# A decode-attention kernel: row loads at the start, the output weights at the end of the stream, fewer score matmuls, and prefetch two heads ahead

## The chip, the cores and the metric

The kernel runs on one core of one Trainium2 chip. The metric is the device time of a run in microseconds (us), as the median of several runs. The profile shows one execution of the same program; its span, from the first to the last instruction, is about 1 to 2 us shorter than the time of the run.

Engines in the profile: PE is the matmul engine and PEld its weight loads, DVE is VectorE, ACT is ScalarE, SP is the engine that issues most DMA transfers. DMA is done by 16 DMA engines, each of which carries a part of every large transfer.

## The reference

One token attends to a long cache, and a small gated MLP ("mixer") is mixed in. Shapes: 32 heads, 16384 cached positions, head size 128, model size 512, all bf16.

```python
q = (x @ wq).reshape(1, 1, 32, 128).transpose(0, 2, 1, 3)
scores = einsum('bhqd,bhkd->bhqk', q, k_cache) * 128 ** -0.5
o = einsum('bhqk,bhkd->bhqd', softmax(scores), v_cache)
a = o.transpose(0, 2, 1, 3).reshape(1, 1, 4096) @ wo
b = mixer(B_x, w_in, w_sp, b_sp, w_out)      # gelu, layernorm, two small products
g = sigmoid((x * gate_w).sum(-1, keepdims=True))
return g * a + (1 - g) * b
```

The two caches are 134 MB each and are read once. There is one query row, so almost no arithmetic is done per byte.

## The kernel before

Each head has a k tile and a v tile of 128 x 16384 bf16 (4.19 MB): partition p holds 128 positions. Scores are made on VectorE and PE together: VectorE multiplies half a k tile by q in place, PE sums over the head size by streaming the products past an identity matrix (16 matmuls of 512 columns per half), and VectorE adds up the last 8 columns. ScalarE takes the exponential. Attention is 128 one-column matmuls with v as weights.

```python
    x_col = const.tile([P, DC], BF16, name="x_col")
    gw_col = const.tile([P, DC], BF16, name="gw_col")
    nc.scalar.dma_start(out=x_col[:], in_=A_x.rearrange("b s (c p) -> p (b s c)", p=P))   # 2-byte pieces
    nc.scalar.dma_start(out=gw_col[:], in_=gate_w.rearrange("(c p) -> p c", p=P))
    ...
    def scores(h):
        ...
        for s in range(2):
            ks = k3[:, s * NH:(s + 1) * NH, :]
            nc.vector.tensor_tensor(out=ks, in0=ks, in1=qh, op=ALU.mult)
            s_ps = ps_s.tile([P, NH, W], FP32, name="s_ps")
            for i in range(NS):                                   # NS = 16
                nc.tensor.matmul(s_ps[:, :, :], lhsT=ident[:, :], rhs=ks[:, :, i * W:(i + 1) * W], ...)
            nc.vector.tensor_reduce(out=s_sb[...], in_=s_ps[:, :, :], axis=AX.X, op=ALU.add)
    ...
    def attend(h, dst):
        for j in range(NJ):                                       # NJ = 128
            nc.tensor.matmul(dst, lhsT=v3[:, j, :], rhs=p_sb[h][:, j:j + 1], ...)

    for h in range(H):          # k and v: two buffers each; k one head ahead
        ...
        if h == 6:
            nc.sync.dma_start(out=wo[:], in_=A_wo.rearrange("(h p) n -> p h n", p=P))
        scores(h)
        if h < last:
            attend(h, o_ps[:, h:h + 1])
    ...                          # softmax sums; o_sb = o * g / sum
    for h in range(last):
        nc.tensor.matmul(a_ps[:, :], lhsT=o_sb[:, h:h + 1], rhs=wo[:, h, :], ...)   # 512 columns each
    attend(last, o31_ps[:, :])
    ...                          # scale, one more wo matmul, copy, store
```

(Cuts are marked by dots.)

The softmax here doesn't subtract the row's maximum and nothing guards it: scores larger than these inputs give would overflow.

## Time and profile before

| | before |
|---|---|
| time, median of 6 runs | 686.27 us (685.47 to 688.01) |
| span of the profiled run | 683.7 us |
| bytes moved | 280.3 MB |
| PE busy, VectorE busy | 424 us (62%), 330 us (48%) |

The first view is the table of stretches: for each stretch its length, then busy time and count of PE, PEld, DVE, ACT and POOL, the granted PE clock (1.00 is full speed), the DMA share (mean busy share of the 16 DMA engines) and GB/s.

```profile
0.00:20.00 20.00, 0.00 (x0) 0.10 (x1) 0.81 (x6) 1.28 (x1) 0.70 (x6) 1.00 0.94 365
20.00:40.00 20.00, 0.00 (x0) 0.00 (x0) 0.00 (x0) 0.00 (x0) 0.00 (x0) 1.00 0.99 421
40.00:50.00 10.00, 5.01 (x20) 2.00 (x20) 2.45 (x3) 1.40 (x4) 0.00 (x0) 1.00 0.98 380
50.00:60.00 10.00, 10.00 (x48) 4.48 (x46) 7.76 (x3) 4.21 (x6) 0.00 (x0) 1.00 0.54 210
200.00:600.00 400.00, 255.58 (x3328) 144.32 (x3328) 204.36 (x82) 8.45 (x42) 0.00 (x0) 0.72 1.00 430
620.00:640.00 20.00, 13.04 (x160) 7.19 (x160) 10.73 (x5) 0.40 (x2) 0.00 (x0) 0.67 0.91 379
660.00:665.00 5.00, 4.33 (x134) 3.53 (x131) 0.64 (x1) 0.00 (x0) 0.00 (x0) 1.00 0.85 345
665.00:670.00 5.00, 3.44 (x9) 1.34 (x10) 0.85 (x4) 0.40 (x2) 0.00 (x0) 0.56 0.15 61
670.00:683.70 13.70, 10.54 (x154) 5.58 (x152) 0.84 (x2) 0.00 (x0) 0.00 (x0) 0.75 0.00 1
```

In the middle the DMA share is 1.00 at 430 GB/s while PE and VectorE have time to spare. At 50 to 60 us the DMA is half idle, and after 670 us there is no DMA.

The list of waits (who waited for whom: us in total, times, longest) names the cause of the first hole, and the timeline of PE (start, length, instruction, count, idle time before it) shows the end.

```profile
PE g_ps L109 <- DMA gw_col<-in_gate_w_dram: 45.0, 1, 45.0
```

```profile
667.19 9.44 PE L233 MATMUL a_ps<-wo,o_sb 128*1 128x512 bf16 x31 [0.95 <-DVE o_sb L231]
676.56 3.40 PE L203 MATMUL o_ps<-p_t,v_t 128*128 128x1 bf16 x128
680.21 0.58 PE L238 MATMUL a_ps<-wo,o 128*1 128x512 bf16 x1 [0.25 <-DVE o L237]
```

The first matmul of the kernel waited 45 us for a load of 1 KB in two-byte pieces, and everything else on PE stood behind it. At the end, 9.4 us of wo matmuls and 3.4 us of attention run when the stream is over.

Three groups of instructions carry the argument about scores (line, engine, operation, shapes, count, then busy us and mean ns, then the idle time before them):

```profile
L191 PE MATMUL s_ps<-k_t,ident 128*128 128x512 bf16 x1024 | 291.3, 454 | 166.2 <-DVE k_t L188 166.2
L188 DVE TENSOR_TENSOR k_t<-k_t,qb 128x8192 bf16<-128x8192 bf16 x64 | 280.4, 4421 | 148.9 <-DMA k_t<-in_A_k_cache_dram 148.8
L193 DVE TENSOR_REDUCE s_sb<-s_ps 128x64 f32<-128x512 f32 x64 | 44.2, 691 | 138.4 <-PE s_ps L191 138.3
```

### The profile page before, as it was taken

The numbers are of one execution on the slowest core, as the hardware profiler recorded it, in microseconds if no ns is written. First come the engines' busy times: TensorE is split into PE (matmuls) and PEld (weight loads), VectorE is DVE, ScalarE is ACT, GpSimd is POOL, SyncE is SP. The second block draws the span as 40 slices with busy tenths as digits, with TensorE's granted clock in tenths as the row PEclk, the third lists the DMA queues.
The fourth block names the chain that finished last, engine by engine and source line by source line (L and its number), as shares of the span: only waits on it lengthen the run. The fifth ranks groups of instructions, "written<-read, shape, count | busy, mean of one in ns | idle before, by whom it ended". The sixth has DMA issues, their size and how long they took to land.

```text
span 683.7 us, 11025 instructions
## 1 busy us (share of the span) xinstructions
PE 424.2 (62%) x5255; PEld 233.8 (34%) x5255; DVE 330.1 (48%) x157; ACT 24.1 (4%) x80; POOL 0.7 (0%) x6
## 2 busy tenths in 40 slices
PE   0038788776176665566666665676665666666677
PEld 0014444432132333333333333343333333333343
DVE  0028565455055555443555554345555543555650
ACT  0012200000000000000000000000000000000000
POOL 0000000000000000000000000000000000000000
PEclk9998676676576677767677677776777667777796
DMA  8998999999999999999999999999999999999980
GB/s 339 431 372 336 428 436 429 436 428 392 438 433 430 430 430 432 427 436 430 429 426 428 427 430 428 429 431 430 432 430 431 430 428 434 428 429 388 417 367 2
DMA packets 17119, 280.29 MB, mean 410 GB/s; under 512 B 2481, under 2 KB 7474, under 8 KB 8242
## 3 DMA queue, kind: packets, MB, share of 16 engines
q1 hardware_dynamic: 15730, 279.58, 96.0%
q8 instruction: 41, 0.67, 0.4%
q10 hardware_dynamic: 1344, 0.00, 0.1%
q14 instruction: 4, 0.03, 0.0%
HBM read 279.58 MB, written 0.00 MB: 409 GB/s over the span
## 4 chain that ended last, share of the span: by engine, by line
DMA 59%; PE 27%; DVE 12%; issue 1%; ACT 0%; SPq 0%; ACTq 0%; DVEq 0%
DMA k_t<-in_A_k_cache_dram 52%; PE s_ps L191 23%; DVE k_t L188 11%; DMA gw_col<-in_gate_w_dram 6%; PE o_ps L203 1%; PE a_ps L233 1%; PE q_ps L121 1%; PE a_ps L176 0%; DVE s_sb L193 0%; SPq L78 0%; ACT L145 0%; ACT p_t L196 0%; DVE res L241 0%; PE ltot_ps L225 0%; PE tot_ps L153 0%
## 5 line engine op out<-in xcount | busy, mean ns | idle before, releaser
L191 PE MATMUL s_ps<-k_t,ident 128*128 128x512 bf16 x1024 | 291.3, 454 | 166.2 <-DVE k_t L188 166.2
L188 DVE TENSOR_TENSOR k_t<-k_t,qb 128x8192 bf16<-128x8192 bf16 x64 | 280.4, 4421 | 148.9 <-DMA k_t<-in_A_k_cache_dram 148.8
L191 PEld LDWEIGHTS <-ident 128*128 128x128 bf16 x1024 | 115.2, 113 | 330.4 <-issue 209.9
L203 PE MATMUL o_ps<-p_t,v_t 128*128 128x1 bf16 x4096 | 109.1, 164 | 38.6 <-ACT p_t L196 38.6
L203 PEld LDWEIGHTS <-v_t 128*128 128x128 bf16 x4096 | 109.2, 98 | 51.7 <-issue 48.0
L193 DVE TENSOR_REDUCE s_sb<-s_ps 128x64 f32<-128x512 f32 x64 | 44.2, 691 | 138.4 <-PE s_ps L191 138.3
L196 ACT ACTIVATE p_t<-s_sb 128x128 bf16<-128x128 f32 x32 | 9.9, 309 | 574.4 <-DVE s_sb L193 574.4
L109 PE MATMUL g_ps<-gw_col,xb 128*128 128x1 bf16 x4 | 0.2, 166 | 45.0 <-DMA gw_col<-in_gate_w_dram 45.0
L109 PEld LDWEIGHTS <-xb 128*128 128x128 bf16 x4 | 0.3, 107 | 44.9 <-issue 27.7
L164 DVE CAST wbf<-wb 128x2 f32<-128x2 bf16 x1 | 0.2, 169 | 30.0 <-DMA wb<-in_B_b_sp_dram 30.0
L233 PE MATMUL a_ps<-wo,o_sb 128*1 128x512 bf16 x31 | 9.4, 478 | 1.0 <-DVE o_sb L231 1.0
L121 PE MATMUL q_ps<-wq_t,xb 128*128 128x512 bf16 x32 | 8.6, 429 | 0.0
L106 DVE COPY xb<-x_col 128x128 bf16<-128x128 bf16 x4 | 0.6, 222 | 15.8 <-DMA x_col<-in_A_x_dram 15.8
L237 DVE TENSOR_TENSOR o<-o_ps,rl 128x1 bf16<-128x1 f32 x1 | 0.2, 160 | 12.9 <-PE o_ps L203 12.9
L196 ACT ACTIVATION_READ_ACCUMULATOR p_t<-s_sb 128x1 f32 x32 | 6.0, 186 | 0.0
L233 PEld LDWEIGHTS <-o_sb 128*1 128x1 bf16 x31 | 3.0, 100 | 7.0 <-issue 3.8
L121 PEld LDWEIGHTS <-xb 128*128 128x128 bf16 x32 | 3.4, 108 | 4.8 <-issue 2.2
L176 PE MATMUL a_ps<-w_out,u 128*1 128x512 bf16 x7 | 3.3, 618 | 2.3 <-DVE u L173 2.3
L126 ACT CAST qb<-q_ps 128x512 bf16<-128x512 f32 x7 | 4.1, 585 | 4.7 <-PE q_ps L121 4.7
L196 ACT ACT_TABLE_LOAD x2 | 2.6, 1283 | 17.6 <-DVE s_sb L193 17.6
L153 PE MATMUL tot_ps<-stats,ones_f 128*128 128x2 f32 x2 | 0.6, 362 | 2.0 <-DVE stats L151 2.0
L176 PEld LDWEIGHTS <-u 128*1 128x1 bf16 x7 | 0.5, 100 | 3.3 <-DVE u L173 2.4
(43 smaller groups left out, 16.3 us busy)
## 6 DMA issues: line engine op xcount, KB each, us to landing
k_t<-in_A_k_cache_dram SPq DMA_DIRECT2D x32, 4096.0 KB, 25.4
v_t<-in_A_v_cache_dram SPq DMA_DIRECT2D x31, 4096.0 KB, 29.8
wq_t<-in_A_wq_dram SPq DMA_DIRECT2D x1, 4096.0 KB, 13.7
wo<-in_A_wo_dram SPq DMA_DIRECT2D x1, 4096.0 KB, 40.8
v_t<-in_A_v_cache_dram SPq DMA_DIRECT2D x1, 2048.0 KB, 24.8
w_in<-in_B_w_in_dram SPq DMA_DIRECT2D x1, 1792.0 KB, 31.4
v_t<-in_A_v_cache_dram SPq DMA_DIRECT2D x1, 1024.0 KB, 27.5
v_t<-in_A_v_cache_dram SPq DMA_DIRECT2D x2, 512.0 KB, 28.1
```

What stands on the lines that cost most here:

```text
L106: nc.vector.tensor_copy(out=xb[:, c, :], in_=x_col[:, c:c + 1].broadcast_to([P, P]))
L109: nc.tensor.matmul(g_ps[:, :], lhsT=xb[:, c, :], rhs=gw_col[:, c:c + 1], start=(c == 0), stop=(c == DC - 1))
L121: nc.tensor.matmul(q_ps[:, :], lhsT=xb[:, c, :], rhs=wq[:, c, nb * QB:(nb + 1) * QB], start=(c == 0), stop=(c == DC - 1))
L126: nc.scalar.copy(out=qb[:, nb * QB:(nb + 1) * QB], in_=q_ps[:, :])
L153: nc.tensor.matmul(tot_ps[:, :], lhsT=ones_f[:, :], rhs=stats[:, :], start=True, stop=True)
L176: nc.tensor.matmul(a_ps[:, :], lhsT=u[:, c:c + 1], rhs=w_out[:, c, :], start=(c == 0), stop=False, skip_group_check=True)
L188: nc.vector.tensor_tensor(out=ks, in0=ks, in1=qh, op=ALU.mult)
L191: nc.tensor.matmul(s_ps[:, :, :], lhsT=ident[:, :], rhs=ks[:, :, i * W:(i + 1) * W], start=(i == 0), stop=(i == NS - 1))
L193: nc.vector.tensor_reduce(out=s_sb[:, s * NH:(s + 1) * NH], in_=s_ps[:, :, :], axis=AX.X, op=ALU.add)
L196: nc.scalar.activation(out=p_t[:], in_=s_sb[:], func=ACT.Exp, scale=inv_sqrt_dh, accum_out=L_sb[:, h:h + 1])
L203: nc.tensor.matmul(dst, lhsT=v3[:, j, :], rhs=p_sb[h][:, j:j + 1], start=(j == 0), stop=(j == NJ - 1))
L233: nc.tensor.matmul(a_ps[:, :], lhsT=o_sb[:, h:h + 1], rhs=wo[:, h, :], start=False, stop=False, skip_group_check=True)
```

## The change

It does five things: (1) x, gate_w and two scalars come as single rows and are spread over the partitions by small matmuls; (2) wq, w_in, w_out and wo are laid out so that each partition reads one long line; (3) VectorE adds the two halves of the head before the identity matmuls, which halves them; (4) k runs two heads ahead in three buffers; (5) wo is loaded last, in five pieces, behind the last v, and is used as weights in one-column matmuls. Small moves go with these: the gate and the mixer come one head earlier in the program, and the last v takes a k buffer and comes in three pieces instead of four.

```diff
-        nc.scalar.dma_start(out=x_col[:], in_=A_x.rearrange("b s (c p) -> p (b s c)", p=P))
-        nc.scalar.dma_start(out=gw_col[:], in_=gate_w.rearrange("(c p) -> p c", p=P))
+    nc.scalar.dma_start(out=x_row[:], in_=A_x.rearrange("b s d -> (b s) d"))
+    nc.scalar.dma_start(out=gw_row[:], in_=gate_w.rearrange("(a d) -> a d", a=1))
 ...
-    nc.sync.dma_start(out=wq, in_=A_wq.rearrange("(c p) n -> p c n", p=P))
+    nc.sync.dma_start(out=wq_t[:], in_=A_wq.rearrange("(p c) n -> p (c n)", c=DC))
 ...
-        t = kv.tile([P, NJ * Dh], BF16, name="k_t", tag="k")
+        t = kv.tile([P, NJ * Dh], BF16, name="k_t", tag="k", bufs=3)
 ...
+        nc.tensor.matmul(xb_ps[:, c * P:(c + 1) * P], lhsT=x_row[0:1, c::DC], rhs=ones_row[0:1, :], ...)
 ...
-            for i in range(NS):
+            nc.vector.tensor_tensor(out=ks[:, :, 0:Dh // 2], in0=ks[:, :, 0:Dh // 2],
+                                    in1=ks[:, :, Dh // 2:Dh], op=ALU.add)
+            for i in range(NS // 2):
 ...
+    AHEAD = 2
+    scores(0)
+    scores(1)
     for h in range(H):
+        if h + AHEAD < H:
+            if h > 0:
+                load_k(h + AHEAD)
+            scores(h + AHEAD)
+        if h > 0:
+            load_v(h, cuts=(64, 96) if h == H - 1 else ())
+        if h < H - 1:
+            attend(h)
 ...
+    wo_src = A_wo.rearrange("(p k) n -> p (k n)", k=H)
+    for a, b in ((0, 12), (12, 20), (20, 26), (26, 30), (30, 32)):
+        nc.sync.dma_start(out=wo_t[:, a * D:b * D], in_=wo_src[:, a * D:b * D])
 ...
-    for h in range(last):
-        nc.tensor.matmul(a_ps[:, :], lhsT=o_sb[:, h:h + 1], rhs=wo[:, h, :], ...)
-    attend(last, o31_ps[:, :])
+    attend(H - 1)
+    ...                                  # two small transposes put o into wo's row order
+    for k in range(H):
+        for c in range(DC):
+            nc.tensor.matmul(a_ps[:, c:c + 1], lhsT=wo4[:, k, c, :], rhs=o2[:, k:k + 1], ...)
+    ...                                  # one small transpose, copy, store
```

## The prediction

> **What bounds the kernel now.** The DMA. The table of stretches shows about 430 GB/s and a DMA share of 1.00 from 200 to 600 us, with PE busy 62 to 65%, VectorE 51%. The Trainium skill ("DMA: Bandwidth & Descriptors", "Where 436 GB/s comes from") puts the ports' ceiling at 435 GB/s; the trace agrees within about 1%. The bytes do not change: 280 MB at 430 GB/s need 652 us. The span is 683.7 us, so about 32 us are lost:
> 1. Start, about 10 us. The two-byte gathers are slow (x_col lands after 16.1 us, gw_col after 43.6). The first matmul waits for gw_col until 45.0 us (list of waits), q follows, the big buffers stay full, and DMA falls to 67 GB/s in 50 to 55 us.
> 2. Middle, about 3 us: 402 GB/s in 160 to 180 us (wo in 1 KB pieces), 349 in 630 to 640.
> 3. End, about 18 us. DMA is done by about 666 us; then follow 9.4 us of wo matmuls, 3.4 us of attention, small work, 2.2 us of output.
>
> The chain of waits says 59% DMA, 27% PE, 12% VectorE; in the middle that is a buffer-recycling loop hidden behind the full DMA queue.
>
> **What the change does.**
> - Start: rows of 1 KB instead of gathers. q starts when wq lands (about 14 us), done by about 23, when k0 lands. scores(0) frees its buffer near 40 us, needed near 59. The hole vanishes: minus 7 us.
> - Middle: wo leaves it, lines become longer: minus 1 to 3 us.
> - End: wo comes last, behind v31. Attention of head 31 and the transposes hide under its 9.7 us (4.19 MB at 430). After its last piece: 8 one-column matmuls (27 ns each, from attention's 109.1 us for 4096), two copies, a transpose, the output: about 4 us instead of 18, minus 14 us.
> - Scores: 512 matmuls of 512 columns go (145 us of PE, off the critical path). VectorE gets 64 adds of 128x4096. A 128x8192 multiply takes 4.42 us, a tiny op 0.15, so an add is an estimated 2.3 us, again two elements per cycle ("VectorE: DVE Perf Modes", "The perf-mode tier table"; the multiply agrees). Plus 147 us: VectorE about 475 us, 72%. Per head 2 x (4.42 + 2.29 + 0.69) = 14.8 us, plus up to 3.5 us waiting for the second half's matmuls: 18.3 us, against 19.5 us of DMA per head. Hidden, with little slack.
> - Prefetch: k runs two heads ahead in three buffers: robustness, no bandwidth, as the queue was never dry in the middle.
>
> **Sum.** 652 us of streaming + 3 start + 1 for small pieces at the end + 4 after the last byte = 660 us span; run times are about 1 to 2 us above the span: **661 us**, 0.963 of before. Range 656 to 671 us. Chances: faster 0.88, same 0.08, slower 0.04.
>
> **What would show it.** DMA share about 1.0 from 5 us until the last 6 us, no slice between under 400 GB/s; first q matmul at 14 to 15 us; adds of 2.2 to 2.4 us; last DMA landing about 4 us before the end; VectorE near 475 us, its idle before multiplies still ended by k loads.
>
> **What would make it wrong.** If VectorE runs multiply, add, wait, reduce strictly in series (2 x 11 = 22 us per head), or attention gets between a head's score matmuls, VectorE passes 19.5 us per head and sets the pace: 700 us or more. Adds at one element per cycle (4.4 us) would do the same. If the deeper queue lifts the rate to 435, about 653 us.

## The result

| | before | after |
|---|---|---|
| time, median | 686.27 us (16 runs, 685.47 to 688.45) | 663.78 us (8 runs, 663.70 to 664.11) |
| span of the profiled run | 683.7 us | 662.4 us |
| PE busy | 424 us | 306 us |
| VectorE busy | 330 us | 472 us |
| bytes moved | 280.3 MB | 280.2 MB |

The 16 runs of the kernel before contain the 6 above. The ratio is 0.9668, 95% interval 0.9657 to 0.9679. Here and below a ratio is the mean time of one kernel's fast runs over the mean of the other's from the same rounds, so it is not quite the ratio of the medians that are quoted. 661 was predicted, within 656 to 671.

The table of stretches of the kernel after, columns as before:

```profile
0.00:20.00 20.00, 7.30 (x29) 3.21 (x30) 2.33 (x10) 3.62 (x5) 0.70 (x6) 1.00 0.94 392
20.00:40.00 20.00, 7.21 (x34) 2.96 (x33) 17.16 (x7) 4.55 (x7) 0.00 (x0) 0.74 0.98 423
40.00:50.00 10.00, 3.33 (x8) 1.09 (x8) 10.00 (x7) 0.40 (x2) 0.00 (x0) 0.83 1.05 452
50.00:60.00 10.00, 4.88 (x13) 1.68 (x13) 10.00 (x5) 0.40 (x2) 0.00 (x0) 0.69 1.00 423
200.00:600.00 400.00, 184.78 (x3013) 111.98 (x3012) 293.32 (x123) 8.57 (x42) 0.00 (x0) 0.63 1.00 430
640.00:650.00 10.00, 5.46 (x202) 5.29 (x198) 0.20 (x1) 0.00 (x0) 0.00 (x0) 0.54 1.00 414
650.00:655.00 5.00, 3.14 (x91) 2.88 (x91) 0.60 (x3) 0.00 (x0) 0.00 (x0) 0.50 0.58 237
655.00:660.00 5.00, 2.96 (x81) 2.52 (x81) 0.16 (x1) 0.00 (x0) 0.00 (x0) 0.50 0.27 104
660.00:662.40 2.40, 0.08 (x1) 0.00 (x0) 0.21 (x1) 0.00 (x0) 0.00 (x0) 0.50 0.00 0
```

The hole at 50 to 60 us is gone and the middle still runs at 430 GB/s. But from 650 us the DMA runs at half and then at a quarter of its rate for 9 us. That was not predicted.

The groups that answer to those of before, with the adds (L217) as a new one:

```profile
L220 PE MATMUL s_ps<-k_t,ident 128*128 128x512 bf16 x512 | 183.1, 535 | 328.8 <-DVE k_t L217 328.8
L215 DVE TENSOR_TENSOR k_t<-k_t,qb 128x8192 bf16<-128x8192 bf16 x64 | 280.4, 4421 | 56.1 <-DMA k_t<-in_A_k_cache_dram 56.1
L217 DVE TENSOR_TENSOR k_t<-k_t 128x4096 bf16<-128x4096 bf16 x64 | 143.7, 2283 | 0.0
L222 DVE TENSOR_REDUCE s_sb<-s_ps 128x64 f32<-128x512 f32 x64 | 44.1, 691 | 87.0 <-PE s_ps L220 87.0
```

An add takes 2.28 us, as estimated, and the multiplies still wait for k loads, though less (56 us instead of 149).

The end, on PE's timeline:

```profile
639.43 2.46 PE L232 MATMUL o_ps<-p_t,v_t 128*128 128x1 bf16 x90
644.26 3.57 PE L232 MATMUL o_ps<-p_t,v_t 128*128 128x1 bf16 x128 [2.37 <-issue]
650.46 1.17 PE L232 MATMUL o_ps<-p_t,v_t 128*128 128x1 bf16 x38 [2.62 <-issue]
653.05 1.42 PE L278 MATMUL a_ps<-o,wo_t 128*128 128x1 bf16 x48 [0.28 <-DVE o L275]
655.40 1.01 PE L278 MATMUL a_ps<-o,wo_t 128*128 128x1 bf16 x32 [0.93 <-DMA wo_t<-in_A_wo_dram]
657.28 0.80 PE L278 MATMUL a_ps<-o,wo_t 128*128 128x1 bf16 x24 [0.86 <-DMA wo_t<-in_A_wo_dram]
658.54 1.01 PE L278 MATMUL a_ps<-o,wo_t 128*128 128x1 bf16 x24 [0.47 <-DMA wo_t<-in_A_wo_dram]
659.81 0.27 PE L283 MATMUL rT_ps<-ident,res_col 128*4 128x128 bf16 x1 [0.25 <-DVE res_col L281]
```

The wo matmuls now follow the arrival of wo's pieces, and 3.3 us lie between the last landing (659.1 us) and the end of the span.

Why does the DMA thin out? A transfer reports one completion per DMA engine, and the trace has the time of each. The 16 completions of the last piece of wo in the kernel after, sorted (us from the start of the span):

```
first eight:  650.73 650.76 650.80 650.90 651.08 651.29 651.53 652.94
last eight:   656.80 656.89 656.99 658.55 658.58 658.62 658.62 659.13
```

Half of the DMA engines are done some four to eight us before the other half. Over the run the spread between the first and last completion of one transfer grows: 0.9 us for a transfer that lands at 56 us, 2.4 at 128, 4.0 at 285, 6.9 at 492, 8.4 at the end. The queue is never dry, so the early half runs ahead, and the late half decides when the stream ends. The kernel before has the same drift (0.6 us at 50 us, 8.1 at 638 us) but only 3.9 us at its end: across its DMA dip at 620 to 640 us the spread falls from 8.1 us (landing at 638 us) to 3.3 us (landing at 648 us), so the late half caught up there.

The drift goes in steps, and the trace shows what they follow. Besides the data it has DMA packets of kind "instruction", in which the engines fetch their instructions: 38 of 16 KB on one queue (q8) and, within the span, four of 8 KB on another (q14). For some transfers of the kernel after: first completion (us), packets of 16 KB and of 8 KB that had started by then, and by how much the late completions came after the first (us):

```
 57.73   0, 0   none late, all 16 within 0.86
 67.43   1, 0   2.42, the other 15 within 0.50
 77.14   2, 0   1.91 2.41, the others within 0.48
106.29   3, 1   1.45 1.90 1.99 2.41, the others within 0.43
183.97   8, 1   1.44 1.70 1.78 1.89 1.90 1.94 1.96 2.01 2.44, the others within 0.40
193.69   9, 1   1.44 1.70 1.77 1.90 1.90 1.93 1.97 2.00 3.98, the others within 0.39
```

Each 16 KB packet makes one completion about 1.5 us later, and it stays late in all transfers that follow. Eight packets hit eight different completions (the ninth late value, 1.44, is of the 8 KB packet), and the ninth packet hits one of the eight for the second time (3.98). Five such turns and the 0.9 us of the beginning make the 8.4 us of the end.

### The profile page after: what moved, and what is told of

Read it like the earlier page. It is cut to its first block, busy times and chain, and to the rows that moved or that the text cites. A ratio compares the mean times of both kernels' runs of the same rounds, so it can differ in the third digit from the quotient of the medians.

```text
span 662.4 us, 10310 instructions
## 1 busy us (share of the span) xinstructions
PE 305.7 (46%) x4875; PEld 185.6 (28%) x4875; DVE 471.5 (71%) x227; ACT 25.5 (4%) x81; POOL 0.7 (0%) x6
## 2 busy tenths in 40 slices
DMA packets 10714, 280.24 MB, mean 423 GB/s; under 512 B 1198, under 2 KB 1200, under 8 KB 1712
## 4 chain that ended last, share of the span: by engine, by line
DMA 61%; DVE 23%; PE 14%; SPq 1%; issue 0%; ACT 0%; DVEq 0%
DMA k_t<-in_A_k_cache_dram 55%; DVE k_t L215 17%; PE s_ps L220 9%; DVE k_t L217 5%; PE o_ps L232 5%; DMA v_t<-in_A_v_cache_dram 3%; DMA wo_t<-in_A_wo_dram 3%; DVE s_sb L222 0%; SPq L87 0%; PE z_ps L163 0%; PE tot_ps L180 0%; SPq L68 0%; PE a_ps L278 0%; ACT rstd L188 0%; DVE z2n L193 0%
## 5 line engine op out<-in xcount | busy, mean ns | idle before, releaser
L220 PE MATMUL s_ps<-k_t,ident 128*128 128x512 bf16 x512 | 183.1, 535 | 328.8 <-DVE k_t L217 328.8
L220 PEld LDWEIGHTS <-ident 128*128 128x128 bf16 x512 | 65.4, 128 | 434.5 <-issue 413.8
L217 DVE TENSOR_TENSOR k_t<-k_t 128x4096 bf16<-128x4096 bf16 x64 | 143.7, 2283 | 0.0
L278 PE MATMUL a_ps<-o,wo_t 128*128 128x1 bf16 x128 | 4.2, 166 | 2.6 <-DMA wo_t<-in_A_wo_dram 2.3
L278 PEld LDWEIGHTS <-wo_t 128*128 128x128 bf16 x128 | 3.9, 104 | 2.9 <-DMA wo_t<-in_A_wo_dram 2.8
L163 PEld LDWEIGHTS <-w_in 128*128 128x128 bf16 x56 | 3.2, 153 | 0.5 <-issue 0.5
L163 PE MATMUL z_ps<-xb,w_in 128*128 128x1 bf16 x56 | 3.1, 192 | 0.0
```

The lines of the kernel that those rows point to most:

```text
L163: nc.tensor.matmul(z_ps[:, fc:fc + 1], lhsT=w_in5[:, c, fc // FhC, :, fc % FhC], rhs=xb[:, c, 0:1], start=(c == 0), stop=(c == DC - 1))
L217: nc.vector.tensor_tensor(out=ks[:, :, 0:Dh // 2], in0=ks[:, :, 0:Dh // 2], in1=ks[:, :, Dh // 2:Dh], op=ALU.add)
L278: nc.tensor.matmul(a_ps[:, c:c + 1], lhsT=wo4[:, k, c, :], rhs=o2[:, k:k + 1], start=False, stop=(k == H - 1), skip_group_check=True)
```

## The experiments

Two sets of questions: is the gain made up as predicted (start, end, nothing from the adds, nothing from the prefetch, VectorE nearly full), and what makes half of the DMA engines late? All kernels below gave the correct result. Experiments ran on the same chip with the kernel before, which had medians of 687.0 to 687.7 us there. The kernel after was measured where the kernel before had 686.27 us, so a comparison of medians with its 663.8 us can be wrong by about 1 us; the ratios are the safer guide.

### 1. b_start: the kernel before with only the start changed

```diff
-        nc.scalar.dma_start(out=x_col[:], ...)      # and gw_col, wb: gathers and broadcasts
+    nc.scalar.dma_start(out=x_row[:], ...)          # and gw_row, wb_row: single rows
+    ... matmuls with a row of ones spread x_row, gw_row, wb_row over the partitions
```

> The kernel before with only its start changed: one-row loads of x, gate_w and the two scalars, spread over the partitions by small matmuls; no other layout, order or size changes. Theory (the prediction's sum): the 67 GB/s hole at 50 to 55 us goes, minus 7 us, about 679 us (677 to 681), ratio about 0.990. Rival: the time saved at the start comes back later, because the loop of two k buffers sets the pace: no more than 2 us gained, 684 us or more.

Measured: 681.97 us, ratio 0.9928 (0.9911 to 0.9945): 5 us instead of 7. The table of stretches of this run:

```profile
0.00:20.00 20.00, 7.88 (x32) 3.37 (x33) 1.93 (x7) 3.02 (x6) 0.70 (x6) 1.00 0.95 390
20.00:40.00 20.00, 14.29 (x117) 6.74 (x115) 10.14 (x4) 4.28 (x8) 0.00 (x0) 0.81 0.98 423
40.00:50.00 10.00, 4.75 (x72) 2.81 (x70) 7.53 (x2) 0.00 (x0) 0.00 (x0) 0.50 1.03 394
50.00:60.00 10.00, 8.30 (x82) 4.14 (x80) 3.64 (x10) 2.27 (x5) 0.00 (x0) 0.84 1.04 445
```

Rate times length, summed, gives 24.65 MB by 60 us against 21.62 MB before: 3.0 MB, or 7.0 us at 430 GB/s. So the hole was worth what was predicted, but alone the edit keeps only 5 us of it. The last landing came at 662.5 us against 667.7 before, also about 5 us. Part of the rest is lost where wo is still loaded in 1 KB pieces: from 100 to 200 us this run moves 420 GB/s, the kernel before 427, and b_both, which has no wo there, 430. Against the kernel before that is 1.6 us. The lines of b_start and then of b_both:

```profile
100.00:200.00 100.00, 56.97 (x781) 32.70 (x779) 41.30 (x18) 2.01 (x10) 0.00 (x0) 0.71 1.01 420
```

```profile
100.00:200.00 100.00, 65.67 (x814) 36.55 (x813) 51.41 (x21) 2.01 (x10) 0.00 (x0) 0.73 1.00 430
```

### 2. b_end: the kernel before with only the end changed

```diff
-        if h == 6:
-            nc.sync.dma_start(out=wo[:], ...)
+    for a, b in ((0, 12), (12, 20), (20, 26), (26, 30), (30, 32)):      # after the last v
+        nc.sync.dma_start(out=wo_t[:, a * D:b * D], in_=wo_src[:, a * D:b * D])
+    ... attention of the last head, transposes and one-column wo matmuls as in the change
```

> The kernel before with only its end changed: wo comes last, in pieces, behind the last v, as in the change, with one-column matmuls and the small transposes. Theory: the 18 us after the last byte become about 4, minus 13 to 15 us: 671 to 674 us, ratio about 0.98. Rival: the last transfers are uneven between the DMA engines or wait for buffers, and half of it is lost: 677 us or more.

Measured: 672.96 us, ratio 0.9792 (0.9777 to 0.9806), which is 14.3 us of 687.1. The last landing stays where it was (667.6 us), and the time after it falls from 16.0 to 3.2 us (span 670.8 us). The stretch in which the stream ends:

```profile
665.00:670.00 5.00, 2.17 (x55) 1.65 (x52) 0.37 (x2) 0.00 (x0) 0.00 (x0) 0.50 0.10 39
```

### 3. b_both: both edits

> The two edits together, still with 16 matmuls and no add per half of scores, two k buffers, one head ahead. Theory: start and end are all of the gain, the adds and the third k buffer give none: 663 to 667 us, as the kernel after (663.8). Rival: the prefetch (three buffers, two heads ahead) or the fewer matmuls carry part of it: 670 us or more.

Measured: 666.09 us, ratio 0.9692 (0.9678 to 0.9707). Start and end together give 21 us, two more than their sum (0.0072 + 0.0208 = 0.0280 against 0.0308), and all but about 2 us of the whole gain. The half-widths of the three intervals (0.0014 to 0.0017) could nearly account for the difference; the tables of stretches point to wo, whose 1 KB pieces slow the stream from 100 to 200 us in b_start (420 GB/s) and are gone from there in b_both (430), 2.3 us at 430 GB/s.

### 4. a_noadd: the kernel after with the old scores

```diff
-            nc.vector.tensor_tensor(out=ks[:, :, 0:Dh // 2], ... op=ALU.add)
-            for i in range(NS // 2):
+            for i in range(NS):
```

> The kernel after with only the scores put back: 16 matmuls and no add per half. Theory: VectorE and PE are both hidden behind the DMA, so 663 to 665 us; VectorE busy about 328 us instead of 472, PE busy about 420 instead of 306. Rival: the halved matmuls shortened something on the critical path, 667 us or more; or the adds cost time, 661 us or less.

Measured: 665.24 us, ratio 0.9680 (0.9665 to 0.9694), with VectorE 331 and PE 414 us busy. The main statement holds (108 us of PE and 141 us of VectorE change place and the time hardly moves), but the kernel is 1.4 us slower than the 663.8 us of the kernel after (0.8 us by the ratios), and its span is 1.0 us longer. The intervals of the two ratios overlap, so this is a hint only. The completions say more: its last landing is at 660.1 us, 0.9 later, and the spread of its last piece is 9.55 us instead of 8.4. What differs for the DMA? The instruction packets of 16 KB: 42 of them here, 38 in the kernel after.

### 5. a_probe and a_probe2: which DMA engines are late

Tiny loads with few rows are queued near the end of the stream (a_probe behind wo; a_probe2 between the last v and wo).

```diff
+    for n, at in ((1, 0), (2, 32), (4, 64), (8, 96)):                   # a_probe
+        nc.sync.dma_start(out=probe[at:at + n, :], in_=A_wo[0:n, 0:256])
+    for i, n in enumerate((6, 8, 10, 12, 14, 15)):                      # a_probe2
+        nc.sync.dma_start(out=probe[i * 16:i * 16 + n, :], in_=A_wo[0:n, 0:256])
```

> The kernel after with four tiny loads (1, 2, 4 and 8 rows of 512 B) queued behind the last piece of wo, to see which DMA engines finish late. In the trace of the kernel after the 16 completions of the last wo piece fall into two groups, eight near 650.7 to 653 us and eight near 656.8 to 659 us. The Trainium skill (DMA: Bandwidth & Descriptors, how many engines a copy uses) says that a copy of 1, 2, 4, 8 rows runs on the lowest-numbered 1, 2, 4, 8 engines. Theory A: the late eight are engines 8 to 15, then all four tiny loads land near 651 to 653 us, before the last piece of wo. Theory B: the late eight are engines 0 to 7, then all land near 657 to 660 us. Mixed: some of both. The time stays within 1 us of 664.

> The kernel after with six tiny loads of 6, 8, 10, 12, 14 and 15 rows between the last v and wo, and the last v and wo in one piece each. The first probe showed 1, 2 and 4 rows done with the early group and of 8 rows six early and two late, so the late engines are a mixture, with none in 0 to 3. This run is for the map: which of the engines 4 to 15 are late. Expected: of the 8 rows six land about 4 to 8 us before the other two; most of the landings that 10, 12, 14 and 15 rows add are late. The time is about 1 to 8 us above 664, as wo in one piece is used later.

Measured: 664.16 and 666.88 us, one run each, on two different chips. The Trainium skill ("DMA: Bandwidth & Descriptors", "Why a DMA increments its semaphore by 16 and not by 1") says that a small copy runs on the lowest-numbered k engines, where k follows from its row count, and that each engine used counts once. The traces agree about the count: 1, 2, 4, 6, 8, 10, 12, 14 and 15 rows gave as many completions, besides one update of the semaphore some 0.4 us after each issue, which is left out here. In a_probe the loads of 1, 2 and 4 rows landed with the early group (by 653.0 us), and of 8 rows the last two came late (656.9 and 657.3 us). In a_probe2 (us):

```
 6 rows: 640.8 640.8 641.4 641.8 642.7 | 647.2
 8 rows: 640.6 641.0 641.0 641.6 642.0 642.9 | 647.0 647.4
10 rows: 640.6 640.8 641.1 641.2 641.8 642.2 643.1 | 647.2 647.6 649.0
12 rows: 640.7 641.0 641.3 641.3 641.9 642.4 643.3 | 647.4 647.8 648.6 649.0 649.2
14 rows: 640.9 641.2 641.5 641.5 642.1 642.6 643.5 | 647.1 647.1 647.6 648.0 648.7 649.1 649.4
15 rows: 641.1 641.5 641.7 641.7 642.3 642.8 643.7 | 647.3 647.3 647.4 647.8 648.2 648.9 649.3 649.6
```

By that numbering the late engines are one of 4 and 5, one of 6 and 7, one of 8 and 9, and 10 to 14: eight. The expectation that engines 8 to 15 would be late fell. The map rests on these two runs (that none of 0 to 3 is late comes from a_probe, the rest from a_probe2); the numbers of the engines themselves are the skill's, the trace does not name them. The wo load in one piece in a_probe2 also answers another question: its last byte landed at 658.6 us, against 659.1 us in five pieces, so the pieces are not what makes the end thin.

### 6. a_instr: more PE instructions, spoilt

```diff
+            if j % 2 == 1 and h < H - 1:
+                nc.tensor.matmul(junk_ps[:, :], lhsT=ident[:, :], rhs=ident[:, 0:1], start=True, stop=True)
```

> The kernel after with 64 meaningless one-column matmuls per head added for PE (1984 of them, about 3970 instructions more), in time in which PE is idle. Putting back the 16 matmuls per half cost 1.4 us (960 instructions more), though neither PE nor VectorE was the limit, and the late engines were about 1.1 us later. Theory: instructions are fetched through the same 16 DMA engines (the profile's queue of kind instruction moved 38 packets of 16 KB, about 1.07 us each), and these fall on the late engines; 3970 instructions are about 15.5 packets more, 16.6 us of one engine: if shared by the eight late engines, about 2 us more, and if by four of them about 4 us; the spread at the end grows by the same. Rival: PE or its clock does it; the matmuls use about 1.7 us of PE per head, which is idle more than half of the time, so nothing changes, 664 us; the spread stays 8.4 us.

Measured: 705.40 us, ratio 1.0269 (1.0235 to 1.0304). Neither theory. The added matmuls wait for nothing, and the scheduler that orders the program put them at the start; PE's timeline shows it:

```profile
11.08 3.56 PE L236 MATMUL junk_ps<-ident 128*128 128x1 bf16 x128 [2.52 <-issue]
17.00 3.55 PE L236 MATMUL junk_ps<-ident 128*128 128x1 bf16 x128 [2.37 <-issue]
24.30 2.60 PE L236 MATMUL junk_ps<-ident 128*128 128x1 bf16 x92 [3.74 <-issue]
```

They delayed q, and with it all buffers. The run says nothing of the late engines. It shows by accident that PE stops every 128 matmuls (256 instructions with their weight loads) for about 2.4 to 3.7 us, although these matmuls need no data. Each stop lies around an instruction packet: the three packets end at 9.69, 15.57 and 22.98 us, and PE goes on 1.3 to 1.4 us later (11.08, 17.00 and 24.30 us).

### 7. a_instr2: the same, tied to its head

```diff
-                nc.tensor.matmul(junk_ps[:, :], lhsT=ident[:, :], rhs=ident[:, 0:1], start=True, stop=True)
+                nc.tensor.matmul(junk_ps[:, :], lhsT=v3[:, j, :], rhs=p_sb[h][:, j:j + 1], start=True, stop=True)
```

> The earlier run with more PE instructions was spoilt: its extra matmuls waited for nothing, and the build placed nearly all of them before and among the q matmuls, at the start. Here the 64 extra matmuls per head read the v tile and the exponentials, so they stay within the attention of their head (checked in the built order). PE gets 3968 instructions more, about 15.5 fetches of 16 KB, spread over the run. Theory (fetches lengthen the late DMA engines): 2 us more if shared by eight engines (666 us), up to 5.8 us if the 1.4 us of the run without adds (960 instructions) is the measure (669.5 us); the spread of the last piece grows by as much. Rival: the fetches do not matter, 664 us and a spread of 8.4 us.

Measured: 669.50 us, ratio 0.9738 (0.9712 to 0.9765), 5.7 us more than the kernel after by the medians, 5.6 by the spans and 4.8 by the ratios, with 53 instruction packets of 16 KB instead of 38. The number is the upper one expected, but not for the reason that was given for it. The last landing moved by 2.3 us only (661.4 us), which is the lower figure, that of eight engines sharing the fetches, but a dip of the DMA has its share in that. The spread did grow while the stream was full, to 9.8 us for the transfer whose first completion is at 621.0 us (8.4 in the kernel after at that time). Then the DMA thinned (402 GB/s between 600 and 640 us), the late half caught up to 5.6 us by 635 us, as in the kernel before, and the last piece had 6.7 us. Why the DMA thinned there was not followed up. The other 3.3 us are PE:

```profile
653.52 0.83 PE L233 MATMUL o_ps<-p_t,v_t 128*128 128x1 bf16 x26
656.97 2.88 PE L233 MATMUL o_ps<-p_t,v_t 128*128 128x1 bf16 x102 [2.62 <-issue]
661.26 3.82 PE L282 MATMUL a_ps<-o,wo_t 128*128 128x1 bf16 x128 [0.28 <-DVE o L279]
```

In the middle of the last head PE stops for 2.62 us and waits for nothing that its own instructions show. The same gaps stand in the kernel after (2.37 and 2.62 us, above), 128 matmuls apart, and not where a piece of v ends (pieces end at matmuls 64 and 96, the gaps come after 90 of a head). The instruction packets tell what PE waits for. The four traces a_instr, a_instr2, a_ahead1 and the kernel after have 26 stops of PE of over 1 us that no wait explains; every one of them ends 1.3 to 1.6 us after an instruction packet of 16 KB has ended (here the packet of 654.41 to 655.49 us, and PE goes on at 656.97). Here the stops make the attention end at 659.9 us, so that the wo matmuls run in one block as the last piece lands (661.4 us), 6.5 us before the end instead of 3.3.

### 8. a_wide: far fewer PE instructions

Attention with four columns of exponentials as weights and 512 columns of v streaming: 32 matmuls per head, one copy, and four small matmuls that pick the diagonal blocks.

```diff
-        for j in range(NJ):
-            nc.tensor.matmul(o_ps[:, h:h + 1], lhsT=v3[:, j, :], rhs=p_sb[h][:, j:j + 1], ...)
+        for g in range(NJ // 4):
+            nc.tensor.matmul(w_ps[:, :], lhsT=p_sb[h][:, 4 * g:4 * g + 4],
+                             rhs=vtile[h][:, 4 * g * Dh:4 * (g + 1) * Dh], ...)
+        nc.scalar.copy(out=w_sb[:], in_=w_ps[:, :])
+        for a in range(4):
+            nc.tensor.matmul(o_ps[:, h:h + 1], lhsT=w_sb[:, a * Dh:(a + 1) * Dh], rhs=ident[0:4, a:a + 1], ...)
```

> The kernel after with attention built from fewer, wider matmuls: four columns of the exponentials are the weights and 512 columns of v stream past them, 32 matmuls per head instead of 128 of one column, then one copy on ScalarE and four small matmuls that pick the four diagonal blocks. PE has about 3860 instructions instead of 9750, so about 16 or 17 instruction fetches of 16 KB instead of 38. In all runs so far the durations of these fetches repeat with a period of eight, so eight engines take turns: five fetches on the busiest engine become two or three. Theory (fetches are what makes eight engines late): 2 to 3 times 1.07 us, the spread of the last landing falls from 8.4 us to 5 to 6 us, and the time from 663.8 to 661 to 662 us. Rival 1: the late engines are slower for another reason; the spread stays about 8 us and the time about 664. Rival 2: PE, which now streams 32 x 512 columns more per head (6.8 us at full clock, 13.7 at half), sets the pace: 668 us or more.

Measured: 664.42 us, ratio 0.9667 (0.9653 to 0.9681): no gain. Yet the theory's own signs are all there. The parts of the page on DMA queues, first of the kernel after and then of this one (queue, kind: packets, MB, share of 16 engines):

```profile
q8 instruction: 38, 0.62, 0.4%
```

```profile
q8 instruction: 15, 0.25, 0.1%
```

The spread of the last piece is 3.1 us instead of 8.4, and the last landing comes at 654.2 us, 5.0 us earlier than in the kernel after. The first completion of that piece comes as before (651.0 against 650.7 us), so all of the 5.0 us is the smaller spread. The stream ends earlier, and PE gives it back:

```profile
648.20 6.21 PE L232 MATMUL w_ps<-v_t,p_t 128*4 128x512 bf16 x28
655.12 0.25 PE L238 MATMUL o_ps<-ident,w_sb 4*128 4x1 bf16 x4 [0.72 <-ACT w_sb L236]
656.71 3.42 PE L284 MATMUL a_ps<-o,wo_t 128*128 128x1 bf16 x128 [0.28 <-DVE o L281]
```

Wide matmuls take longer for one head (7.1 us of PE instead of 3.4), so the last head ends at 654.4 us, after the last landing, and its small chain and all 128 wo matmuls follow: 8.8 us after the last byte instead of 3.3.

Gains and losses are of equal size only by chance. A version with wide attention for all heads but the last two should have both the early landing and the short tail: an estimate of 654.2 + 3.3 = 657.5 us span, about 659 us. It was not run.

### 9. a_dve2 and a_dve3: how much room VectorE has

```diff
+            nc.vector.tensor_tensor(out=ks[:, 0:64, Dh // 2:Dh], in0=ks[:, 0:64, Dh // 2:Dh],
+                                    in1=ks[:, 0:64, Dh // 2:Dh], op=ALU.mult)         # a_dve2: + 2.28 us per half
+            nc.vector.tensor_tensor(out=ks[:, 0:48, Dh // 2:Dh], ...)                 # a_dve3: + a second one
```

> The kernel after with a second VectorE operation of the size of the add (128x4096, 2.28 us) per half, into columns that nobody reads. VectorE then needs 14.6 + 4.6 = 19.2 us per head without waits, and about 22 with the 2.7 us per head that it waits for PE in the kernel after. Theory: over the 19.5 us of DMA per head VectorE sets the pace, 700 to 730 us. Rival: waits shrink and it stays at 664 to 672 us.

Measured: 664.10 us (one run). The theory fell: 64 more operations of 2.28 us on VectorE (606 us busy instead of 472) cost nothing.

> The kernel after with two extra VectorE operations per half (2.28 and about 1.75 us). One such operation cost nothing: its 4.56 us per head filled the 2.7 us of waits for PE and the 1.75 us of waits for k. VectorE now needs 2 x (4.42 + 2.28 + 2.28 + 1.75 + 0.68) = 22.8 us per head without any wait, over the 19.5 us of DMA. Theory: VectorE sets the pace: 23 us of start + 32 x 22.5 + about 10 us of end = 750 us (740 to 765). Rival: something else gives, under 700 us.

Measured: 750.17 us (one run), as expected. Stretch 200 to 600 us, of a_dve2 and then of a_dve3:

```profile
200.00:600.00 400.00, 186.14 (x3024) 112.69 (x3024) 390.90 (x169) 8.45 (x42) 0.00 (x0) 0.64 1.00 430
```

```profile
200.00:600.00 400.00, 160.03 (x2592) 96.13 (x2592) 400.00 (x182) 7.57 (x38) 0.00 (x0) 0.62 0.92 382
```

At 391 of 400 us busy VectorE is still hidden and the DMA still gets 430 GB/s; at 400 of 400 it sets the pace. The waits for PE (87 us in the kernel after) do not add to the work: when more work is there, it stands in the place of the wait. In a_dve2 the reductions do not wait at all.

```profile
L224 DVE TENSOR_REDUCE s_sb<-s_ps 128x64 f32<-128x512 f32 x64 | 43.6, 681 | 0.0
```

### 10. a_ahead1: one head of prefetch, two k buffers

```diff
-        t = kv.tile([P, NJ * Dh], BF16, name="k_t", tag="k", bufs=3)
+        t = kv.tile([P, NJ * Dh], BF16, name="k_t", tag="k")
-    AHEAD = 2
+    AHEAD = 1
```

> The kernel after with one head of prefetch and two k buffers instead of two heads and three; wo gets a tile of its own, the last v a v buffer. Theory: the queue is never dry with either, so 663 to 666 us. Rival: the third buffer is what keeps the DMA busy, 670 us or more (with the adds VectorE holds a k buffer longer).

Measured: 665.15 us, ratio 0.9681 (0.9664 to 0.9697). The last landing is where it was (658.9 against 659.1 us). The profiled span is 0.9 us longer because PE stops among the last wo matmuls, 1.5 us after the end of an instruction packet (657.64 us) until 659.11 us:

```profile
655.50 2.41 PE L273 MATMUL a_ps<-o,wo_t 128*128 128x1 bf16 x85 [0.28 <-DVE o L270]
659.11 1.31 PE L273 MATMUL a_ps<-o,wo_t 128*128 128x1 bf16 x43 [1.20 <-issue]
```

So the third buffer does not feed the DMA better.

## Why the prediction was right

**"What bounds the kernel now. The DMA."** Right, before and after: 430 GB/s from 200 to 600 us in both. The Trainium skill ("DMA: Bandwidth & Descriptors", "Where 436 GB/s comes from") gives a ceiling of 435 GB/s for the ports, and none of the 100 us stretches of these two runs from 100 to 600 us went over it (at most 432); for loads from HBM the same section names a lower limit of a core, about 358, which the one core that ran here passes with its 430.

**Start, "minus 7 us".** The mechanism is right: without the gathers 7.0 us worth of bytes more had moved by 60 us (b_start). Alone it kept 5 us in the time. The first q matmul started at 13.3 us, a little before the 14 to 15 that were named.

**Middle, "minus 1 to 3 us".** About right: with wo in 1 KB pieces 100 to 200 us ran at 427 GB/s before (420 in b_start), without it at 431, which is 0.9 us (2.6) of streaming.

**End, "minus 14 us".** Right: b_end gained 14.3 us.

**Scores, "off the critical path".** Right in size (adds of 2.28 us, which agrees with the perf-mode table of the skill's page "VectorE: DVE Perf Modes", section "The perf-mode tier table": 4096 elements at two per cycle; VectorE 472 us busy). Undoing it cost 1.4 us by the medians, 0.8 by the ratios. That small cost has a source that the prediction did not think of: fewer matmuls are fewer instructions to fetch (38 packets instead of 42).

**"18.3 us, against 19.5 us of DMA per head. Hidden, with little slack."** Hidden, but the slack was wrong. The step that failed is the sum "14.8 us, plus up to 3.5 us waiting for the second half's matmuls": a wait is room, not work. a_dve2 put 4.56 us more per head on VectorE at no cost; the limit shows only where work alone exceeds 19.5 us (a_dve3, 22.8 us per head, 750 us).

**Prefetch, "robustness, no bandwidth".** Right for the DMA (a_ahead1).

**The sum.** Predicted: 652 of streaming, 3 start, 1 "for small pieces at the end", 4 after the last byte. Measured in the kernel after: 280.24 MB at 430 GB/s are 651.7 us; the first 20 us moved 392 x 20 = 7.84 MB, which is 18.2 us of streaming, so the start cost 1.8; the last landing was at 659.1, which leaves 659.1 - 651.7 - 1.8 = 5.6 us for the thin end; and 3.3 us followed it. The mis-sized term is the third: 5.6 us instead of 1. It is not the small pieces (in one piece wo landed no later, a_probe2) but the drift of half of the DMA engines, which the prediction did not have. The other terms were 1.2 and 0.7 us too large and by luck hid part of it.

**Signs that were wrong.** "DMA share about 1.0 until the last 6 us": it fell at 650 us, 12 us before the end. The "middle" loss at 630 to 640 us in the kernel before was partly no loss: while the early engines were idle, the late ones caught up.

**What makes the engines late.** The instruction fetches. Three things show it. First, the steps: in each trace one completion steps back for each packet and stays back. Added up over the 16 completions, and up to about 621 us (630 in the kernel before), where nothing had yet caught up, the lateness grew by 1.4 us per packet in the kernel after (38 packets of both sizes), 1.35 in a_wide (17), 1.5 in a_instr2 (51), a_noadd (41) and the kernel before (41). Second, the count was changed on purpose: fewer packets (15 of 16 KB instead of 38) brought the spread of the last piece from 8.4 to 3.1 us and the last landing forward by 5.0 us; more (53) made the spread 9.8 us before the dip and the last landing 2.3 us later. Third, the turns: the durations of successive instruction packets repeat with a period of eight, and eight completions are late.

```
kernel after, us:  1.073 1.069 1.060 1.108 1.100 1.087 1.018 1.026 | 1.081 1.069 1.069 1.099 1.099 1.086 1.018 1.018
```

The trace does not name the engine of a packet, so that the fetches take turns over these eight engines is read from the steps. Open is why a packet of 1.07 us makes its engine 1.4 to 1.5 us later.

## What to carry to other kernels

When a kernel is bound by DMA, count three things apart: the bytes at the sustained rate, the time before the stream runs, and the time after its last byte; here the last two were the whole gain, and 118 us less on PE gave almost nothing. A wait of an engine in the middle of a stream is room for more work, so compare its work per turn with the DMA's time per turn, not its work plus its waits. If the queue never runs dry, look at the completions of one transfer engine by engine at the end: half of the engines can be late, each instruction fetch makes one of them later (about 1.4 us a packet here), and what comes last should need few instructions and little work after it.

## What the Trainium skill lacked or had wrong

- "Runtime: NRT & Kernel Launch", section "Instruction fetch mechanics", says that instructions come in blocks of 16 KB (256 instructions) through a DMA queue and that crossing a block is "mostly hidden". The block size agrees (38 packets of 16 KB). Under a saturated DMA it was not hidden: most packets took 1.02 to 1.11 us, PE stood still for 2.4 to 2.6 us at intervals of 256 instructions within the last heads and went on 1.3 to 1.5 us after an instruction packet had ended, and 15 packets' worth of instructions more (a_instr2, with their matmuls) cost about 5 us of 664.
- No page that was read says that these fetches seem to rotate over eight of the 16 DMA engines (period of eight in the durations), or that each makes one engine about 1.4 us later for good in a stream that never runs dry: 8.4 us of 659 with 38 packets, 3.1 us of 654 with 15.
- "DMA: Bandwidth & Descriptors", section "Latency and other measured facts", calls engines 7 and 15 usually slower than the rest (the reason that it guesses belongs to another way of issuing DMA, with descriptors made on GpSimd). By the probes here eight were late, engine 15 (the 16th, by the skill's numbering) was not among them, and of 6 and 7 one was; the traces do not say which.
